# Moving the w turns, scans and gammas of units 4 and 5 into the first group's steps (RWKV-7 state recurrence with a hard-swish feed-forward)

## The chip, the cores and the metric

The kernel runs on one core of one Trainium2 chip. The metric is the device time of one execution in microseconds, the median of several runs.

## What is computed

The reference runs an RWKV-7 recurrence over 4 batches of 8 heads, 768 steps, head dimension 40, and puts its output through a two-layer feed-forward:

```python
for t in range(S):                       # state: (B, H, D, D), 0 at first
    y[:, :, t] = einsum('bhd,bhde->bhe', r_t, state)
    Sa = einsum('bhde,bhe->bhd', state, a_t)
    state = state * w_t[:, :, None, :] - einsum('bhd,bhe->bhde', Sa, b_t) \
            + einsum('bhd,bhe->bhde', v_t, k_t)
x = y as (B*S, H*D) = (3072, 320)
h = x @ w_in                             # (320, 2048)
out = (h * clip(h + 3, 0, 6) / 6) @ w_out   # (2048, 320)
```

## The kernel before

Time is cut into blocks of 64 steps. A **unit** is 128 rows: one block of two batches, eight heads each. There are 24 units; four of them (NU = 4) make a **group** of 128 steps for all batches. Units 0 to 3 are the first group, 4 to 7 the second.

For each unit `prepare(i, F)` gives the stages that don't need the state:

- `W`: four PE transposes of w into a PSUM bank, two copies of the halves into a tile `wm` (ACT; DVE for unit 0 alone), and a running product by a DVE scan (L544) into `prods`. It then fetches the next w of its tile.
- `gam`: reciprocal, a second DVE scan backwards (L555), and copies (DVE for units of later groups, POOL) that give the decay factors `gam`, their inverses `rgam` and `dec`. For units 4 to 8 it also fetches the unit's own v.
- `A`, `B`, `K`: turns of a, b, k, multiplied by `gam` or `rgam`; `factor`: k and b times the turned `rgam`; `F`, `E`, `EV`: products of these.

The F tiles of the group's units are inverted together, step by step on DVE (`invert`, L741 and L747), with `third_block` products at the end. `step(i)` gives the stages that use the inverse and the state: `RT`, `VT` (turns of r and v), `R`, `C`, `S`, `U`, `UT`, `rS`, `sn` (state update), `H`, `y`, and `move`, `move2`, which send the unit's result to its feed-forward tile `xt` by eight DMAs on SP.

A stage is a Python generator: its PE part is emitted, then it yields, then the rest (emptying the PSUM bank) is emitted. Between the two, other work can be dealt in. Each engine runs its own instructions in the order in which they are emitted; all DMAs spoken of here are emitted on SP's queue.

The w_in and w_out matrices come as 20 **weight pieces** that are converted before use (`load_weights`): per piece one to four load DMAs on SP (L328, into `raw` tiles and borrowed places), three ACT operations (L351, L353, L355) into one of two `parts` buffers, and three DVE operations (L372, L376, and L363, which writes the weight). A raw place can be loaded again only when an earlier piece is converted.

The order around the change is written out by hand. `PLAN` is a list of lines that run the first group's own steps: `2U:3` means stage U of unit 2, with three weight steps dealt between its PE part and the rest. `X` and `Y` are the third-block products of the inverse. From line 8 on, feed-forward **pieces** (`expand`, L1054, and `contract`, L1095) are emitted behind each line, and from line BEGIN = 10 on each line also takes one step of `second_group`, the stages of units 4 to 7 up to EV. `by_twos` deals these: in its step 0 come W of unit 4, W of unit 5, gam of 4, gam of 5, each followed by `pieces(0.625)`; step 1 has nothing; step 2 is A, step 3 is B of units 4 and 5 and W of 6 and 7. The tail of the plan reads:

```python
              3R:4 3VT                      # line 8
              2rS:3 2sn:3 2H:4 3S:2
              2y:3 3U:1 3UT:10 3C:5         # line 10
              3rS:1 3sn:2 3H:4 2move
              3y:1 2move2
```

PSUM tiles come from `ps_any` (a ring with the banks `one`, `pair` and at first `o`) and `ps_pair` (double banks, `pair` and at first `lent`); a stage waits until the last user of its bank has emptied it.

The w of unit 5 is loaded after line 8 into half of a tile (`WA1`) whose memory an earlier weight piece (raw_x) holds, together with its a (`seconds()`). Five tiles `values` hold v; unit i's v goes to `values[i % 5]`, so the fifth is first used by unit 4.

Of the kernel before, what the change touches and what calls it, by code (L numbers as in the profile page):

```python
# [8 lines left out]
F32 = mybir.dt.float32  # L9
# [22 lines left out]
def kernel(  # L32
# [152 lines left out]


    AHEAD = NU + 1
    PADS = {"W": 1.0}

    def padded(t, name):  # L190
        nc.gpsimd.memset(t[:, :, D:SLOT], PADS.get(name, 0.0))
        return t
# [32 lines left out]
        score.append(t)  # L225
    turn = [0]

    values = [padded(const.tile([P, H, SLOT], F32, name=f"V{i}"), "V") for i in range(AHEAD)]
    inputs["R"] = padded(const.tile([P, H, SLOT], F32, name="R"), "R")

    RR = const.tile([P, 2, NPR * D + SLOT - D], F32, name="RR")
# [202 lines left out]
    def fetch(name, i, engine=None):  # L434

        if i is None or i >= NK:
            return
        x, crossed = {"W": (w, 0), "A": (a, 0), "B": (b, 0), "K": (k, 0), "R": (r, 1),
                      "V": (v, 1)}[name]
        if name == "V":  # L440
            t = values[i % AHEAD]
        else:
            t = placed.get((name, i))
            if (name, i) == ("R", 1):
                t = others["K"]
            t = t if t is not None else (others if i < 2 * NU and i % 2 and name != "R" else inputs)[name]
        g, p = names[i]
        engines = engine or nc.sync
        for q in range(2):
            engine = engines[q] if isinstance(engines, tuple) else engines  # L450
            y = x[2 * p + q, :, g * BL:(g + 1) * BL, :]
            rows = slice(q * BL, (q + 1) * BL)
            if crossed:
                for s in range(2):
                    engine.dma_start(out=t[rows, 4 * s:4 * s + 4, 0:D],
                                     in_=y[s::2].rearrange("h t e -> t h e"))
            else:
                engine.dma_start(out=t[rows, :, 0:D], in_=y.rearrange("h t e -> t h e"))
        data[i][name + "N"] = t

    def following(i):

        if i < 2:
            return None
        if i < 2 * NU:

            return i + 2 if i % NU < NU - 2 or i % 2 == 0 else None
        return i + 1
# [55 lines left out]
    def prepare(i, F):  # L524
        n, o = i % NU, data[i]
        halves = i >= 2 * NU
        def w_stage():
            wt = turn_pairs(o["WN"])
            yield PE

            wm = o["wm"] = wms[i % 2]
            wv = wm[:, 0:SCAN].rearrange("p (r m i) -> p r m i", m=2, i=HB + 1)
            x = wt[:].rearrange("p r (q m i) -> p (r q) m i", q=2, m=2)
            if i == 0:
                nc.vector.tensor_copy(wv[:, :, 0, 1:HB + 1], x[:, :, 0, ::-1])
            else:
                nc.scalar.activation(out=wv[:, :, 0, 1:HB + 1], in_=x[:, :, 0, ::-1], func=AF.Copy)
            if i == 0:
                nc.vector.tensor_copy(wv[:, :, 1, 1:HB + 1], x[:, :, 1, :])
            else:  # L540
                nc.scalar.activation(out=wv[:, :, 1, 1:HB + 1], in_=x[:, :, 1, :], func=AF.Copy)  # L541
            fetch("W", following(i))
            prods = o["prods"] = tmp.tile([P, NB, 2, HB + 1], F32, name="prods", bufs=2)
            nc.vector.tensor_tensor_scan(  # L544
                out=prods[:].rearrange("p r m i -> p (r m i)"), data0=wm[:, 0:SCAN], data1=start[:],
                initial=0.0, op0=ALU.mult, op1=ALU.add,
            )

        def gam_stage():

            prods, wm = o["prods"], o["wm"]
            first = start[:].rearrange("p (n i) -> p n i", i=HB + 1)[:, :, 0]
            nc.vector.reciprocal(first, prods[:].rearrange("p r m i -> p (r m) i")[:, ::-1, HB])
            back = _ap(wm[:], SCAN, [[-1, SCAN]])
            nc.vector.tensor_tensor_scan(out=back, data0=back, data1=start[:], initial=0.0,  # L555
                                         op0=ALU.mult, op1=ALU.add)
            nc.vector.memset(first, 1.0)
            gam = o["G"] = grp.tile([P, NPR, P], F32, name="gam", tag="gam", bufs=NU + 2)
            rgam = o["rg"] = placed.get(("rgam", i)) or tmp.tile([P, NPR, P], F32, name="rgam", bufs=2)
            gv = gam[:].rearrange("p r (q i) -> p (r q) i", q=2)  # L560
            rv = rgam[:].rearrange("p r (q i) -> p (r q) i", q=2)
            row = 2 * (HB + 1)

            def copy(to, x):
                if i < NU:
                    nc.scalar.activation(out=to, in_=x, func=AF.Copy)
                else:
                    nc.vector.tensor_scalar(to, x, 1.0, None, ALU.mult)

            copy(gv[:, :, 0:HB], _ap(o["wm"][:], HB + 1, [[row, NB], [-1, HB]]))  # L570
            copy(rv[:, :, HB:BL], _ap(o["wm"][:], HB + 3, [[row, NB], [1, HB]]))
            nc.gpsimd.tensor_copy(gv[:, :, HB:BL], o["prods"][:, :, 1, 0:HB])  # L572
            nc.gpsimd.tensor_copy(rv[:, :, 0:HB], o["prods"][:, :, 0, 0:HB][:, :, ::-1])
            dec = grp.tile([P, 2, 2, NPR], F32, name="dec", tag="dec", bufs=NU + 2)
            nc.gpsimd.tensor_copy(dec[:].rearrange("p m q r -> p r q m"),
                                  o["prods"][:].rearrange("p (r q) m i -> p r q m i", q=2)[:, :, :, :, HB])
            o["dec"] = dec
            if NU <= i <= 2 * NU:
                fetch("V", i)
            yield from ()  # L580

# [120 lines left out]
    def in_turn(stages, order):  # L702

        for name in order:
            yield from stages[name]()
            shared[0] = None
            yield DONE

    def by_stages(i, stages):


        order = ["K", "factor", "F"] if i % NU < 2 else ["K", "F", "factor"]
        return in_turn(stages, ["W", "gam", "A", "B"] + order + ["E", "EV"])


    def invert(F, third, alone=False):
# [435 lines left out]
    def run(stage, steps=0, mixed=0, deals=0):  # L1152

        for at in stage:
            if at == DONE:
                return
            aside(steps, mixed)
            deal(deals)
# [17 lines left out]
    def by_twos(first, steps, mixed, rate):  # L1176


        chains = [by_stages(first + i, prepared(first + i)) for i in range(NU)]
        for t in range(TWOS):  # L1180

            order = [0, 1] if t < STAGES else []
            order += [2, 3] if t > 5 else []
            if t < 2:
                order = [0, 1, 0, 1][4 * t:]
            if t == 3:
                order = [2, 0, 3, 1]
            for i in order:
                run(chains[i], steps if t > 10 else 0, mixed)
                pieces(rate / 2)  # L1190
            if t == 10:
                side.append(invert(group_F[-1], third, first == 0))
            yield
# [16 lines left out]
    for n, x in enumerate(BESIDE):  # L1210
        limit[0] = {0: 4, 8: 12}.get(n, limit[0])
        while n == 0 and refill[0]():
            pass
        if n == 4:
            fetch("R", 0)
            fetch("R", 1)
        run(chains[int(x[0])], 1, MIXED if n >= 12 else 0)
    TURNS_IN = [("one", 1), ("pair", 2), ("pair", 2)]
    blocks = {}
# [26 lines left out]
    def block(i, j):  # L1246

        if i % NU < 2:
            if j == 0:
# [4 lines left out]


    PLAN = """X X:2 0U:4 0UT:2 1R
              0sn:2 0H:1 Y:2
              1U 1UT:2 0y
              2RT:1 Y:1
              1sn:1 1H:1 2VT:2 0move 0move2  # L1260
              1y:2 2R
              2S:3 3RT:2
              1move 1move2 2U:3 2UT:1 2C:5
              3R:4 3VT
# [9 lines left out]
    chains = {str(i): in_turn(stages[i], [x[0][1:] for line in plan for x in line if x[0][0] == str(i)])  # L1274
              for i in range(NU)}
    chains.update({x: firsts[n] for n, x in enumerate("XY")})
    for t, line in enumerate(plan):
        if t == 8:
            begun_ffn()
            ring.clear()  # L1280
            ring.extend([("one", 1), ("whole", 2)])
        for name, *amounts in line:
            run(chains[name[0]], 0, 0, *map(int, amounts))
        if t == 3:
            limit[0] = PIECES
        if t == BEGIN - 2:
            seconds()
            for name in "WA":
                fetch(name, NU + 1)
            third.clear()  # L1290
            second_group = by_twos(NU, 3, 0, 1.25)
        if t == BEGIN + 1:

            for name in "BK":
                others[name] = second(name)
                fetch(name, NU + 1)
        if t >= BEGIN - 2:
            pieces(3 if t < BEGIN else 1.5 if t < BEGIN + 3 else 0)
        if t >= BEGIN:
            next(second_group)  # L1300
# [156 lines left out]
```

## Time and profile before

| | |
|---|---|
| time, median of 3 runs | 798.12 us (797.23 to 798.37) |
| the profiled execution | span 802.0 us; no other time of it is given |
| mean granted TensorE clock | 0.956 |
| PE busy | 733.3 us (91%) |
| DVE busy | 495.5 us (62%) |
| ACT busy | 321.2 us (40%) |
| POOL busy | 175.6 us (22%) |
| L1054 and L1095 on PE, the feed-forward | 250.4 and 231.8 us |
| chain that ended last | PE 77%, DVE 8%, issue 5%, DMA 4%, SP's queue 2% |

All times of the profile are of one execution, counted from its first instruction. A row of the chain gives start, length and the engine and line that the end waited for; a row of the timeline gives start, length, engine, line, operation, output and inputs, and in brackets how long the engine had stood idle before it, with the releaser that the profile infers. "issue" means that the profile shows no releaser. PEld is PE's weight load, SPq the DMAs that SP issues. The first 140 us hold the first group; in them PE is busy 2 to 7 tenths.

### The profile page before, as it was taken

The page shows a single profiled execution, that of the slowest core. Times are in us where ns is not written, and L with a number is a line of the kernel's source. Part 1 is how long each engine was busy: PE and PEld are TensorE (multiplying, and loading weights), DVE is VectorE, ACT ScalarE, POOL GpSimd, SP SyncE. Part 2 cuts the span into 40 slices and gives each one's busy share as a digit, 9 for nine tenths or more (in the row PEclk, how much of TensorE's full clock was granted, in tenths as well). Part 3 has the DMA queues.
Part 4 walks back from the last instruction along what each step waited for, and adds up shares of the span by engine and source line. Part 5 has one row for each costly group of instructions (what it writes and reads, how often), then busy time and mean ns, then how long its engine had stood idle before and what let it go on. Part 6 is the DMA issues. An engine that isn't in the chain of part 4 may idle for free.

```text
span 802.0 us, 35325 instructions
## 1 busy us (share of the span) xinstructions
PE 733.3 (91%) x15832; PEld 622.8 (78%) x15832; DVE 495.5 (62%) x967; ACT 321.2 (40%) x668; POOL 175.6 (22%) x318
## 2 busy tenths in 40 slices
PE   5726777999999989999999999999999999999998
PEld 4625665878778868888888888888888888888886
DVE  7896777679555699455698445897444973322210
ACT  2348882321644424543344453324443324422111
POOL 6403012420322222223123123304122202000000
PEclk9855798999999999999999999999999999999999
DMA  9683553420233331233222233213222101110000
GB/s 120 118 198 85 152 142 57 76 46 9 45 57 66 59 56 28 53 64 56 41 45 43 44 58 62 46 34 57 44 51 48 20 20 29 30 25 13 15 19 17
DMA packets 174215, 45.03 MB, mean 56 GB/s; under 512 B 157424, under 2 KB 172784, under 8 KB 174064
## 3 DMA queue, kind: packets, MB, share of 16 engines
q1 hardware_dynamic: 169760, 42.03, 27.7%
q8 instruction: 125, 2.05, 1.1%
q10 hardware_dynamic: 4304, 0.74, 0.7%
q14 instruction: 26, 0.21, 0.1%
HBM read 34.08 MB, written 3.93 MB: 47 GB/s over the span
## 4 chain that ended last, share of the span: by engine, by line
PE 77%; DVE 8%; issue 5%; DMA 4%; SPq 2%; ACT 2%; POOL 1%; DVEq 0%; ACTq 0%; POOLq 0%
PE h L1054 26%; PE o L1095 24%; PE pair L512 4%; PE pair L972 3%; PE pair L484 2%; PE pair L949 2%; PE one L474 2%; PE pair L894 2%; PE pair L856 2%; PE pair L914 1%; PE pair L690 1%; PE pair L930 1%; DMA R<-in_r_dram 1%; DVE wm L555 1%; PE pair L799 1%
## 5 line engine op out<-in xcount | busy, mean ns | idle before, releaser
L1054 PE MATMUL h<-xt,win 128*128 128x128 f32 (+1 forms) x2304 | 250.4, 282 | 3.5 <-DVE gt L1070 3.5
L1054 PEld LDWEIGHTS h<-xt,win 128*128 128x128 f32 (+1 forms) x2304 | 230.8, 192 | 20.5 <-issue 4.2
L1095 PE MATMUL o<-wout,gt 128*128 128x320 f32 x768 | 231.8, 445 | 0.0
L1095 PEld LDWEIGHTS o<-wout,gt 128*128 128x128 f32 x768 | 139.2, 191 | 51.0 <-issue 1.2
L1070 DVE SCALAR_TENSOR_TENSOR gt<-gt,h 128x512 f32<-128x512 f32 x96 | 62.0, 681 | 71.7 <-ACT gt L1069 71.6
L1069 ACT ACTIVATE gt<-h,three 128x512 f32<-128x512 f32 x96 | 62.2, 686 | 100.9 <-PE h L1054 100.5
L984 POOL TENSOR_TENSOR yg<-ys,gam 128x512 f32<-128x512 f32 x22 | 39.0, 1772 | 165.4 <-DVE ys L983 91.2
L741 DVE TENSOR_TENSOR prod<-x 128x30 f32<-128x30 f32 (+9 forms) x180 | 67.2, 373 | 8.8 <-POOL x L726 3.3
L663 POOL TENSOR_TENSOR KBt<-K,rgt 128x320 f32<-128x320 f32 x22 | 19.0, 865 | 215.4 <-ACT rgt L652 166.9
L747 DVE TENSOR_TENSOR x<-x,prod 128x30 f32<-128x30 f32 (+9 forms) x180 | 62.3, 346 | 5.5
L957 DVE TENSOR_TENSOR state<-pair,state 40x320 f32<-40x320 f32 (+1 forms) x44 | 21.4, 487 | 65.9 <-PE pair L949 39.8
L520 DVE COPY_PREDICATED score<-mask,pair 128x512 f32<-128x512 int32 x71 | 49.9, 723 | 1.8 <-PE pair L512 1.4
L983 DVE TENSOR_TENSOR ys<-pair,ys 128x512 f32<-128x512 f32 x22 | 15.2, 691 | 44.7 <-PE pair L690 22.0
L555 DVE TENSOR_TENSOR_SCAN wm<-wm,start 128x528 f32<-128x528 f32 x24 | 37.6, 1565 | 0.8
L544 DVE TENSOR_TENSOR_SCAN prods<-wm,start 128x528 f32<-128x528 f32 x24 | 30.3, 1270 | 10.2 <-ACT wm L541 10.1
L834 ACT ACTIVATE RT<-pair 128x512 f32<-128x512 f32 x21 | 12.5, 597 | 52.9 <-PE pair L484 52.9
L972 PE MATMUL pair<-score,KBt 64*64 64x64 f32 x1472 | 29.2, 232 | 4.0 <-DVE state L957 3.2
L695 ACT ACTIVATE EV<-pair 64x320 f32<-64x320 f32 x44 | 19.0, 432 | 33.5 <-PE pair L690 22.8
L972 PEld LDWEIGHTS pair<-score,KBt 64*64 64x64 f32 x1472 | 25.8, 145 | 6.6 <-DVE state L957 3.7
L809 ACT ACTIVATE tinv<-pair 32x256 f32<-32x256 f32 x48 | 18.0, 375 | 30.1 <-PE pair L799 29.5
L1113 ACT ACTIVATE ob<-o 128x320 f32<-128x320 f32 x22 | 9.6, 435 | 49.1 <-PE o L1095 29.3
L572 POOL COPY gam<-prods 128x256 f32<-128x256 f32 x24 | 22.5, 937 | 29.3 <-DVE prods L544 25.4
(262 smaller groups left out, 1062.6 us busy)
## 6 DMA issues: line engine op xcount, KB each, us to landing
V<-in_v_dram SPq DMA_DIRECT2D x96, 40.0 KB
out_dram<-ob SPq DMA_DIRECT2D x47, 80.0 KB
R<-in_r_dram SPq DMA_DIRECT2D x92, 40.0 KB
B<-in_b_dram SPq DMA_DIRECT2D x42, 80.0 KB
K<-in_k_dram SPq DMA_DIRECT2D x42, 80.0 KB
W<-in_w_dram SPq DMA_DIRECT2D x37, 80.0 KB
A<-in_a_dram SPq DMA_DIRECT2D x37, 80.0 KB
xt<-yg SPq DMA_DIRECT2D x72, 40.0 KB
```

Source lines behind the costliest of these rows:

```text
L512: nc.tensor.matmul(out=o[i][half(q), n, :], lhsT=lhs[half(i, D), n ^ (2 * q * swap), half(q)], rhs=rhs[half(i, D), n, half(q)], start=True ...
L520: nc.vector.copy_predicated(out=x[:].rearrange("p (i h) t -> p i h t", i=2), mask=mask8, data=o[2])
L544: nc.vector.tensor_tensor_scan(out=prods[:].rearrange("p r m i -> p (r m i)"), data0=wm[:, 0:SCAN], data1=start[:], initial=0.0, op0=ALU.m ...
L555: nc.vector.tensor_tensor_scan(out=back, data0=back, data1=start[:], initial=0.0, op0=ALU.mult, op1=ALU.add)
L741: nc.vector.tensor_tensor(out=pv, in0=_ap(x[:], (i + 1) * L + i, [[L, n], [0, i]]), in1=_ap(x[:], i * L, [[0, n], [1, i]]), op=ALU.mult,)
L747: nc.vector.tensor_tensor(out=rest, in0=rest, in1=pv, op=ALU.add)
L972: nc.tensor.matmul(out=y[q][half(s), pr, :], lhsT=o[name][half(q), h * D:h * D + SLOT], rhs=m[name][half(q), 4 * rs + 2 * s + j, :], start ...
L984: nc.gpsimd.tensor_tensor(out=yg[:], in0=m["ys"][:].rearrange("p r q t -> p r (q t)"), in1=o["G"][:], op=ALU.mult)
L1054: nc.tensor.matmul(out=hp[c][:, i, :], lhsT=lhsT, rhs=rhs, start=(begun[c] == 0), stop=(begun[c] == 3 * NQ - 1))
L1069: nc.scalar.activation(out=gt[:], in_=hp[c][:], func=AF.Relu, bias=three[:], scale=1.0)
L1070: nc.vector.scalar_tensor_tensor(out=gt[:], in0=gt[:], scalar=6.0, in1=hp[c][:], op0=ALU.min, op1=ALU.mult)
L1095: nc.tensor.matmul(out=op[:], lhsT=gts[c][:, n, :], rhs=wout[:, c * HJ + r * NQ + n, :], start=((split or r == 0) and c == 0 and n == 0), ...
```

## The change

- W and gam of units 4 and 5 leave `by_twos` and become two chains, P and Q, in the plan: W of 4 at the end of line 1, gam of 4 at the end of line 2, W of 5 at the end of line 3, gam of 5 at the end of line 5. Step 0 of `by_twos` keeps only its feed-forward pieces.
- The two copies of the W stage of units 4 and 5 are done by DVE and no longer by ACT.
- The w of unit 5 goes into the fifth tile of v, and is loaded early, behind r of units 0 and 1. That tile's padding is therefore 1.0.
- The DMAs move with it: W of unit 6 is fetched in line 1, V of unit 5 in line 5 (with gam of 5). V of unit 4, A of unit 5 and W of unit 7 are fetched after line 8; before, W and A of unit 5 were fetched there, and W of 6 and 7 and V of 4 and 5 in step 0 of `by_twos`.

```diff
-    PADS = {"W": 1.0}
+    PADS = {"W": 1.0, "V4": 1.0}
...
+            if (name, i) == ("W", NU + 1):
+                t = values[NU]
...
-            if i == 0:
+            if i in (0, NU, NU + 1):
                 nc.vector.tensor_copy(wv[:, :, 0, 1:HB + 1], x[:, :, 0, ::-1])
...
-            fetch("W", following(i))
+            if i != NU + 1:
+                fetch("W", following(i))
...
-            if NU <= i <= 2 * NU:
+            if NU < i <= 2 * NU:
                 fetch("V", i)
...
+        scanned = [] if i < NU + 2 else ["W", "gam"]
...
-                run(chains[i], steps if t > 10 else 0, mixed)
+                if t >= 2 or first != NU:
+                    run(chains[i], steps if t > 10 else 0, mixed)
                 pieces(rate / 2)
...
             fetch("R", 1)
+            fetch("W", NU + 1)
...
     PLAN = """X X:2 0U:4 0UT:2 1R
-              0sn:2 0H:1 Y:2
-              1U 1UT:2 0y
-              2RT:1 Y:1
+              0sn:2 0H:1 Y:2 P
+              1U 1UT:2 0y P
+              2RT:1 Y:1 Q
               1sn:1 1H:1 2VT:2 0move 0move2
-              1y:2 2R
+              1y:2 2R Q
...
+    chains.update({x: in_turn(prepare(NU + n, None), ["W", "gam"]) for n, x in enumerate("PQ")})
...
         if t == BEGIN - 2:
             seconds()
-            for name in "WA":
-                fetch(name, NU + 1)
+            fetch("V", NU)
+            fetch("A", NU + 1)
+            fetch("W", NU + 3)
```

More of the change, by code (lines that the diff above doesn't have):

```diff
@@ L226 @@
     turn = [0]
-    values = [padded(const.tile([P, H, SLOT], F32, name=f"V{i}"), "V") for i in range(AHEAD)]
+    values = [padded(const.tile([P, H, SLOT], F32, name=f"V{i}"), f"V{i}") for i in range(AHEAD)]
     inputs["R"] = padded(const.tile([P, H, SLOT], F32, name="R"), "R")
@@ L537, in w_stage @@
                 nc.scalar.activation(out=wv[:, :, 0, 1:HB + 1], in_=x[:, :, 0, ::-1], func=AF.Copy)
-            if i == 0:
+            if i in (0, NU, NU + 1):
                 nc.vector.tensor_copy(wv[:, :, 1, 1:HB + 1], x[:, :, 1, :])
@@ L709, in by_stages @@
     def by_stages(i, stages):
+        scanned = [] if i < NU + 2 else ["W", "gam"]
         order = ["K", "factor", "F"] if i % NU < 2 else ["K", "F", "factor"]
-        return in_turn(stages, ["W", "gam", "A", "B"] + order + ["E", "EV"])
+        return in_turn(stages, scanned + ["A", "B"] + order + ["E", "EV"])
     def invert(F, third, alone=False):
```

## The prediction

> **What bounds the kernel now.** I read the slices of the page first. PE is at nine tenths or more from the eighth slice (140 us) on, with one 8 among them, and at 2 to 7 tenths before it, so what moves from behind that border to before it leaves a full engine for one with room. The change touches 50 to 138 us; I asked for the chain of waits from 60 to 140 us (start, length, what):
>
> ```profile
> 119.92 0.77 ACT parts L351
> ...
> 122.58 0.69 DVE wout L363
> 123.27 0.64 DVE score L520
> 123.92 2.30 DVE prods L544 x2
> ...
> 126.53 1.32 DVE wm L555
> ...
> 128.95 1.26 DVE wm L555
> ...
> 130.74 1.19 DVE gt L1070 x2
> 131.93 0.41 DVE state L957
> ...
> 132.39 1.98 PE pair L972 x64
> 134.37 4.18 PE o L1095 x8
> ```
>
> Two things end last here: the conversion of the feed-forward weights (L351 to L376, the last piece done at 123.27), and then the scans of units 4 and 5 on DVE, 123.92 to 130.74, in front of unit 3's state update, mask and product y. The timeline shows what PE does meanwhile (start, length, engine, line; idle before it in brackets):
>
> ```profile
> 122.10 0.58 ACT L920 ACTIVATE UT<-pair 128x512 f32<-128x512 f32 x1
> 122.77 0.63 PE L474 MATMUL pair<-ident,WA 128*128 128x128 f32 x4 [3.75 <-issue]
> 127.85 1.34 PE L1095 MATMUL o<-wout,gt 128*128 128x320 f32 x4
> 132.39 1.98 PE L972 MATMUL pair<-score,KBt 64*64 64x64 f32 x64 [3.19 <-DVE state L957]
> 134.30 4.25 PE L1095 MATMUL o<-wout,gt 128*128 128x320 f32 x8
> 138.39 0.60 PE L474 MATMUL one<-ident,A 128*128 128x128 f32 x4
> ```
>
> Unit 5's w turn waits 3.75 us until ACT has emptied unit 3's UT out of a `pair` bank (122.68), and ACT does that only after the ten weight steps dealt there. The product y waits 3.19 us for the scans. Eight L1095 then take 4.25 us, where another eight (at 150.56) take 2.42; the windows give a granted clock of 0.50 for 132 to 138 us.
>
> Last, SP's own timeline, because the change moves DMAs into it:
>
> ```profile
> 96.96 2.72 SPq L455 DMA_DIRECT2D R<-in_r_dram  x4
> 99.72 3.10 SPq L998 DMA_DIRECT2D xt<-yg  x4
> 102.87 3.51 SPq L1003 DMA_DIRECT2D xt<-yg  x4
> 106.48 0.52 SPq L328 DMA_DIRECT2D raw<-in_moe_w_out_dram  x1
> 107.11 1.36 SPq L458 DMA_DIRECT2D WA<-in_w_dram  x2
> 108.53 1.58 SPq L458 DMA_DIRECT2D WA<-in_a_dram  x2
> 110.21 1.34 SPq L328 DMA_DIRECT2D raw_fb<-in_moe_w_out_dram  x1
> ...
> 124.76 6.20 SPq L455 DMA_DIRECT2D V<-in_v_dram  x8
> ```
>
> From 81.69 (raw_x) to 113.2 us SP issues back to back, with gaps near 0.1 us. Weight piece 17 (raw_fb) is issued at 110.21, lands 4.51 us later (the chain), and ACT reads it at 115.54: under 1 us to spare.
>
> **What leaves 117 to 131 us.** Were everything earlier unmoved: unit 3's rS follows the emptying of UT, 122.7 + 0.69 = 123.4; sn needs the bank of the mask that ends at 123.92, two products of 0.65, so 125.2; H 0.69, 125.9; the four L1095 1.34, 127.3. Mask and state update, free of 6.8 us of scans, are done by 126.7. Product y starts at 127.3 instead of 132.39 (5.1 us earlier). At full clock y takes 1.69 (as at 112.93) and the eight L1095 2.42, so the turn of unit 4's a starts at 131.5 instead of 138.39: 6.9 us gained. The two turns themselves (0.6 us each) are in that figure. The feed-forward pieces that stood between them stay, 40 matmuls of about 0.13 us, and fill PE's wait. From 138 us PE is nearly solid up to 173 us, so I carry a shift there to the end one for one.
>
> **What arrives at 50 to 97 us.** Unit 5's w load is two DMAs (1.3 us, like L458) behind the R loads near 46 us; what it delays is used much later and the inversion on DVE covers it: 0 (1.3 us if that cover went). On PE: two turns of four at half clock, 0.66 to 1.11 us each (R at 80.28, V at 87.17); the first lies in a stretch that PE fills (72 to 81.9 us), so 1.0; the second can fall into the 2.7 us idle at 81.91. On ACT: nothing, the copies go to DVE, and four of 0.38 us leave ACT at 122.6. POOL gets six copies (0.3 to 1.4 us) in a stretch where it is nearly idle: 0; it loses them at 125 to 129, where unit 5's B and K pads stood behind them.
>
> On DVE per unit: copies 0.42 + 0.42 (rows of unit 0, L535 and L539), scan 1.26, reciprocal 0.25, scan 1.26, memset 0.07, copies 0.28 + 0.29: 4.25, together 8.5 us. Queue by queue in program order: unit 4's copies and scan hide in the 2.0 us idle ahead of L980 at 80.39, which comes 1.0 late through PE. Gam of 4 (2.15) then stands before L372, unit 2's scaling and L376, and unit 5's copies and scan before unit 1's state update: 82.1 + 2.15 + 1.6 + 2.1 = 88.0 against 86.40. The mask of 1H ends near 89.8 instead of 88.14, y and R of units 1 and 2 follow 1.7 late, and gam of 5 (2.15) stands before piece 8's L372: 95.3 instead of 91.27. Piece 8's L363 ends at 97.1, not 93.2; its `parts` buffer is what ACT needs for piece 10 at 94.14 (0.9 to spare): ACT is 3.0 late. The windows give ACT 5.84 to 5.87 us busy of each 6 from 90 to 108 us, so it doesn't catch up; with unit 2's U and UT between, some 3.6 late at the last pieces.
>
> On SP: W of unit 6 (1.3 us) fits the gap before raw_x. raw_x waits for the third block's product on PE, 1.1 late. Then four V DMAs for unit 5 (half of the 6.20 us row: 3.1) come ahead of piece 15, R, unit 1's moves and piece 16; four for unit 4 (3.1) and W of unit 7 in the place of unit 5's (0) ahead of pieces 17 to 19. Full price: 7.3 us; piece 17 lands at 122.0 instead of 114.7, and ACT's last conversions and the UT emptying behind them end 6.5 late. Some of it may be given back: one-DMA weight issues take 0.45 to 0.52 us (pieces 16, 18) but 1.30 and 1.34 at others (15, 17), and single moves 0.57 to 1.63, which suggests up to about 3 us of waiting that is absorbed.
>
> So the end of the conversions, and with it the 6.9 us, is put back by 3.6 (ACT alone) to 6.5 us (SP at full price). I take 5.0, a little nearer to the middle than to SP's end because of the uneven issues. Sum: −6.9 + 5.0 = −1.9 us. Against the profiled execution (span 802.0 us, the only figure of that execution) this is 800.1; the median of the runs, 798.12, is 3.9 below that span, and the shift is taken over unchanged: 796.2.
>
> **Rivals.** *The delay does not bite* (0.19): DVE's scans fall into idle times and SP's issues close up, so the conversions end only 1 to 2 us late; gain 5.5, time 792.6. For it: DVE is busy 2.41 of 6 us at 78 to 84 and 3.43 at 84 to 90. Against it: the back-to-back SP row.
>
> *Slower: the wait is moved ahead of rS and costs the clock* (0.26). If SP's price is paid in full, UT is emptied at about 129.2 (122.68 + 6.5), while PE, with C of unit 3 done near 119.7 (116.6 + about 3) and 40 feed-forward matmuls behind it (5.3), runs out of work near 125.0: 4 us idle in one piece. In this trace the 3.19 us wait at 129.2 was followed by clock 0.50 from 132 to 138, though the 3.75 us at 119 was not (clock 1.00 in the windows to 130). At half clock rS, sn and H (0.69 + 1.30 + 0.69 = 2.7) take 2.7 more: −6.9 + 6.5 + 2.7 = +2.3, 800.4. It decides from a delay of about 5.9 on, where 6.9 − 2.7 − delay leaves −1.6.
>
> The Trainium skill, "TensorE: Matmul & The Clock Gate", Part 1, states that the array falls to half clock after an idle window of about 3.4 us on a free-running clock, so that a wait of this length may or may not cause it. The two waits above, one with and one without a drop, agree with that; by the rule alone an idle of 4 us, given the full SP price, would mostly bring the drop, and the sum would be the 800.4 of this rival.
>
> *The wait only moves* (0.10): the full SP price but no drop of the clock, or a drop with less delay: −0.4, 797.7. That the change doesn't do what it says would look the same, with scans still between 123 and 131 us; the code gives no way to that, so it has no chance of its own.
>
> **How the numbers follow.** A measurement of this kernel can tell about 0.2%, 1.6 us. The forecast (0.45) spans delays of 3.6 to 6.5 us, 794.8 to 797.7, and about 1 us more on either side for the other terms: 0.31 faster, 0.12 same, 0.02 slower. With the rivals 0.19 faster, 0.26 slower and 0.10 same: 0.50, 0.22, 0.28. The range runs from 791.8 (a little beyond the first rival, short of the full 6.9) to 800.9 (just beyond the slower one).
>
> **What would show it.** In the changed kernel: no L544 or L555 between 123 and 131 us, but four pairs' worth between 76 and 96; V issues near 96 and 110 us on SP; raw_fb of L328 issued near 116 instead of 110.21; the last L363 ending near 128, UT (L920) right after it; y of unit 3 (L972) near 132 at the latest with no DVE wait before it; the eight L1095 in 2.4 us if the clock held; unit 4's a turn near 136.5. I am wrong if the conversions end before 125 (gain nearer 5), if PE's idle before rS is followed by clock 0.50 (loss), or if a shift at 138 us is not found again at the end.

## The result: 0.3% slower, and the profile after

| | before | changed |
|---|---|---|
| time, median of 7 runs | 798.21 us (797.23 to 799.13) | 800.35 us (798.94 to 802.92) |
| ratio to before | | 1.0034 (1.0018 to 1.0049) |
| profiled execution | span 802.0 us | span 798.6 us, time 800.6 us |

The changed kernel is slower in time and shorter in the profiled span. Both are true: the execution of before that was profiled was an unusually long one. The changed kernel's own profile puts 2.0 us outside its span; with as much, before's profiled execution took about 804 us, longer than any of its seven runs. The first experiment gives a second profile of before.

The stretch in question, from the timeline of the changed kernel (line numbers are 4 higher from L1054 on; L920 became L924, L930 became L934, y's L972 became L976, and the turns' L474 became L476):

```profile
116.86 4.04 PE L1058 MATMUL h<-xt,win 128*128 128x128 f32 x40
126.79 0.58 ACT L924 ACTIVATE UT<-pair 128x512 f32<-128x512 f32 x1
127.42 1.13 PE L934 MATMUL pair<-RT,S 40*64 40x64 f32 x32 [6.52 <-ACT UT L924]
131.07 2.50 PE L1099 MATMUL o<-wout,gt 128*128 128x320 f32 x4
134.97 2.42 PE L1099 MATMUL o<-wout,gt 128*128 128x320 f32 x8
137.23 0.60 PE L476 MATMUL one<-ident,A 128*128 128x128 f32 x4
```

No scan stands in front of unit 3's y any more, and the eight L1099 run at full speed. But unit 3's UT is emptied only at 126.79. PE has done its 40 feed-forward matmuls by 120.90 and waits 6.52 us in one piece; behind the wait rS (L934) takes 1.13 us and the four L1099 take 2.50, against 0.69 and 1.34 where before runs them at a clock of 1.00 (125.32 and 127.85 in its profile). SP's and ACT's timelines say why UT is late:

```profile
96.33 2.68 SPq L457 DMA_DIRECT2D V<-in_v_dram  x4
109.22 3.36 SPq L457 DMA_DIRECT2D V<-in_v_dram  x4
115.42 0.57 SPq L328 DMA_DIRECT2D raw_fb<-in_moe_w_out_dram  x1
120.28 0.77 ACT L351 ACTIVATE parts<-raw_fb,low 128x512 int32<-128x512 int16 x1 [4.10 <-DMA raw_fb<-in_moe_w_out_dram]
```

The two groups of V loads stand ahead of weight piece 17 on SP; it is issued at 115.42, and ACT stands idle 4.10 us until it lands.

### The profile page after: what moved, and what is told of

Same layout as the page of the kernel before. It is cut to its first block, busy times and chain, and to the rows that moved or that the text cites. A ratio compares the mean times of both kernels' runs of the same rounds, so it can differ in the third digit from the quotient of the medians.

```text
span 798.6 us, 35318 instructions
## 1 busy us (share of the span) xinstructions
PE 731.4 (92%) x15832; PEld 621.3 (78%) x15832; DVE 495.9 (62%) x971; ACT 320.0 (40%) x664; POOL 174.7 (22%) x318
## 4 chain that ended last, share of the span: by engine, by line
PE 72%; DVE 13%; issue 5%; DMA 4%; SPq 4%; ACT 2%; POOL 1%; DVEq 0%; ACTq 0%; POOLq 0%
PE h L1058 24%; PE o L1099 22%; PE pair L514 4%; PE pair L976 3%; DVE prod L745 3%; DVE x L751 3%; PE pair L953 2%; PE pair L486 2%; PE one L476 2%; SPq L460 2%; PE pair L898 2%; SPq L457 2%; PE pair L860 2%; PE pair L934 1%; PE pair L918 1%
## 5 line engine op out<-in xcount | busy, mean ns | idle before, releaser
L1099 PE MATMUL o<-wout,gt 128*128 128x320 f32 x768 | 230.8, 443 | 0.0
L1099 PEld LDWEIGHTS o<-wout,gt 128*128 128x128 f32 x768 | 138.7, 190 | 50.5 <-issue 0.4
L976 PE MATMUL pair<-score,KBt 64*64 64x64 f32 x1408 | 26.2, 223 | 0.2 <-issue 0.2
L864 DVE TENSOR_TENSOR RR<-pair,EV 128x320 f32<-128x320 f32 x22 | 10.7, 486 | 25.3 <-PE pair L514 25.3
```

Source lines behind the costliest of these rows:

```text
L976: nc.tensor.matmul(out=y[q][half(s), pr, :], lhsT=o[name][half(q), h * D:h * D + SLOT], rhs=m[name][half(q), 4 * rs + 2 * s + j, :], start ...
L1099: nc.tensor.matmul(out=op[:], lhsT=gts[c][:, n, :], rhs=wout[:, c * HJ + r * NQ + n, :], start=((split or r == 0) and c == 0 and n == 0), ...
```

## The experiments

All ratios are to the kernel before, run beside them on the same chip. "UT" is the start of the ACT operation that empties unit 3's UT, "a turn" the start of unit 4's a turn on PE, where the dense part begins; both from one profiled execution each.

| kernel | piece 17 issued | UT | a turn | span | ratio (95%) |
|---|---|---|---|---|---|
| before, first profile | 110.21 | 122.10 | 138.39 | 802.0 | |
| e1 before again | 108.52 | 120.28 | 135.79 | 797.2 | 0.9999 (0.9988 to 1.0010) |
| changed | 115.42 | 126.79 | 137.23 | 798.6 | 1.0034 (1.0018 to 1.0049) |
| e8 changed again | 115.43 | 127.11 | 136.89 | 799.1 | 1.0041 (1.0025 to 1.0057) |
| e2 scans early, V late | 110.02 | 122.42 | 132.06 | 792.4 | 0.9951 (0.9931 to 0.9970) |
| e3 V early alone | 116.23 | 127.89 | 141.36 | 803.2 | 1.0061 (1.0043 to 1.0078) |
| e6 V of 5 late only | 113.72 | 124.91 | 135.05 | 797.2 | 0.9988 (0.9972 to 1.0005) |
| e4 A and W late too | 107.87 | 121.91 | 131.50 | 793.9 | 0.9955 (0.9939 to 0.9972) |
| e10 copies on ACT | 110.04 | 122.07 | 131.70 | 794.0 | 0.9957 (0.9940 to 0.9974) |
| e5 gammas at lines 11, 12 | 110.31 | 121.77 | 132.49 | 796.3 | 0.9986 (0.9970 to 1.0002) |
| e7 changed, idle transposes | 116.31 | 127.78 | 135.48 | 797.8 | 0.9999 (0.9984 to 1.0013) |
| e9 e2, idle transposes | 110.77 | 123.99 | 132.05 | 796.9 | 0.9965 (0.9951 to 0.9980) |

**e1, the kernel before again** (no edit).

> The kernel before, unaltered, for a second profile of it. Its first profile has a span of 802.0 us, 3.9 us over the median of its runs, and the profile of the changed kernel a span of 798.6 us in an execution of 800.6 us, 2.0 us of it outside the span. Theory A (the first profile of before was an unlucky execution): the span is near 796 us, the 2.7 us idle of PE at 82 us in the midst of unit 1's sn is missing or much shorter, and unit 3's y (L972) starts 2 to 4 us earlier than 132.39. Theory B (the time around the span differs between the two kernels): the span is again near 802 us with the same stops at the same places. Time: 798.2 us, ratio 1.000 within 0.002 in both.

Its profiled execution took 798.97 us, of it 797.2 in the span: theory A. Its timeline has the same stops, but shorter or earlier (SP's line first):

```profile
108.52 0.57 SPq L328 DMA_DIRECT2D raw_fb<-in_moe_w_out_dram  x1
120.28 0.58 ACT L920 ACTIVATE UT<-pair 128x512 f32<-128x512 f32 x1
130.58 1.34 PE L972 MATMUL pair<-score,KBt 64*64 64x64 f32 x64 [1.66 <-DVE state L957]
135.79 0.60 PE L474 MATMUL one<-ident,A 128*128 128x128 f32 x4
```

PE's stop in unit 1's sn is 1.7 us, not 2.7; y starts 1.8 us earlier than in the first profile (I had said 2 to 4), and the a turn 2.6. Of the 4.8 us between the two spans these are 2.6; the rest is spread over the later part. This execution is the fastest of e1's twelve, 0.8 us under their median, so it is nearer to the middle than the first profile but not at it. Against it the changed kernel's a turn is 1.4 us late, and so is the end of its span.

**e2, scans early, V late**: the turns, scans and gammas as changed; the eight V loads behind line 10.

```diff
-            if NU < i <= 2 * NU:
+            if NU + 1 < i <= 2 * NU:
                 fetch("V", i)
...
-            fetch("V", NU)
             fetch("A", NU + 1)
...
+        if t == BEGIN:
+            fetch("V", NU)
+            fetch("V", NU + 1)
```

> The changed kernel with the eight DMAs of V of units 4 and 5 behind line 10 of the plan, where before has them, and all else as changed. SP theory (the V DMAs put back the last weight pieces, PE then idles 6.5 us before unit 3's rS and falls to half clock): raw_fb of L328 is issued near 110 us instead of 115.4, UT of unit 3 is emptied near 123 instead of 126.8, PE's idle before rS is under 3 us and rS, sn, H run at clock 1.0; time 794 to 796 us, faster than before by 2 to 4 us. DVE theory (the 8.5 us of scans and copies on DVE put back ACT's conversions whatever SP does): UT is still emptied after 125.5 us and the time stays at 799 to 801 us.

```profile
110.02 0.57 SPq L328 DMA_DIRECT2D raw_fb<-in_moe_w_out_dram  x1
122.42 0.58 ACT L924 ACTIVATE UT<-pair 128x512 f32<-128x512 f32 x1
123.05 0.69 PE L934 MATMUL pair<-RT,S 40*64 40x64 f32 x32 [2.17 <-ACT UT L924]
126.28 2.50 PE L1099 MATMUL o<-wout,gt 128*128 128x320 f32 x4
132.06 0.60 PE L476 MATMUL one<-ident,A 128*128 128x128 f32 x4
```

With SP relieved, the same early scans make the kernel 0.5% faster than before (795.0 us, median). The expectation held but for one point: even the 2.17 us wait was followed by half clock, on H and the four L1099.

**e3, V early alone**: before, with only the V loads at the changed kernel's places.

```diff
-            if NU <= i <= 2 * NU:
+            if NU + 1 < i <= 2 * NU:
                 fetch("V", i)
...
+        if t == 5:
+            fetch("V", NU + 1)
         if t == BEGIN - 2:
             seconds()
+            fetch("V", NU)
```

> The kernel before with only the eight V DMAs of units 4 and 5 moved to the places where the changed kernel has them (V of 5 behind line 5, V of 4 behind line 8); turns and scans stay. SP theory: raw_fb is issued 5 to 6 us later than in before, UT of unit 3 is emptied 4 to 5 us later and the whole kernel is 3 to 6 us slower (802 to 804 us). DVE theory: SP's delay is absorbed, 798 to 799 us.

```profile
116.23 0.57 SPq L328 DMA_DIRECT2D raw_fb<-in_moe_w_out_dram  x1
127.89 0.58 ACT L920 ACTIVATE UT<-pair 128x512 f32<-128x512 f32 x1
141.36 0.60 PE L474 MATMUL one<-ident,A 128*128 128x128 f32 x4
```

Piece 17 is issued 7.7 us later than in e1, UT is emptied 7.6 later (both more than expected), and the kernel is 0.6% slower. e2 (−0.49%) and e3 (+0.61%) add up to +0.12%; the whole change measures +0.34% (0.18 to 0.49). The two halves of the change are shown: the move of the scans gains, the move of the V loads loses about as much or a little more. Behind the early scans the V loads cost 0.83% (changed against e2), behind the late ones 0.61%; the intervals do not tell these two apart.

**e6, V of unit 5 late only**: as e2, with V of unit 4 left behind line 8.

> The changed kernel with only V of unit 5 behind line 10; V of unit 4 stays behind line 8. SP theory: raw_fb is issued 2.7 to 3 us earlier than 115.4, near 112.6, it lands near 117.3, piece 17 starts on ACT there, UT is emptied near 123.9 instead of 126.8, and the time lies between e2 (795.0) and the changed kernel (800.4), near 796.5 to 797.5. If the loss came from one of the two alone, it would be at one of the ends.

All places fall between those of e2 and of the changed kernel: piece 17 at 113.72 (1.1 later than I had said), UT at 124.91. The ratio lies between too. A group of four V DMAs takes 2.7 to 3.5 us to issue on SP; at the end of the conversions that of unit 4 costs 2.5 us here (UT against e2), and that of unit 5 another 1.9 (the changed kernel against this one). Here PE waits 4.40 us, and rS takes 1.13 us behind that wait too: the clock dropped with a delay of UT of only 4.6 us against e1.

**e7, the changed kernel with idle transposes**, to part the wait from the clock.

```diff
+        if t == BEGIN:
+            idle = bank("one", [P, 512], 1)
+            for _ in range(48):
+                nc.tensor.transpose(out=idle[:, 0:P], in_=ident[:], identity=ident[:])
```

> The changed kernel with 48 PE transposes of the identity into the free bank of units 4's turn, behind line 10's feed-forward pieces; their result is used by nobody. They fill some 5 us of PE's 6.5 us wait before unit 3's rS and change no other engine's work. Clock theory (the wait costs not only itself but half clock behind it): rS, sn and H take 0.69, 1.3 and 0.69 us instead of 1.13, 2.1 and 1.11, the four L1099 1.34 instead of 2.50, granted clock 1.0 from 126 to 134 us, and the kernel is 1.5 to 2.5 us faster than the changed one, about 798 to 799. If the half clock costs nothing because masks and state update end last there: 800.4 within 0.7.

The windows of the changed kernel, and then of e7, for the same 6 us (busy time of PE, PEld, DVE, ACT and POOL, granted clock, DMA share, GB/s):

```profile
126.00:132.00 6.00, 4.58 (x130) 4.27 (x131) 4.28 (x7) 3.08 (x6) 0.52 (x2) 0.50 0.19 31
```

```profile
126.00:132.00 6.00, 4.44 (x142) 3.54 (x140) 5.24 (x9) 3.94 (x7) 0.51 (x2) 1.00 0.18 29
```

```profile
128.41 0.69 PE L934 MATMUL pair<-RT,S 40*64 40x64 f32 x32 [1.37 <-ACT UT L924]
130.86 1.34 PE L1099 MATMUL o<-wout,gt 128*128 128x320 f32 x4
135.48 0.60 PE L476 MATMUL one<-ident,A 128*128 128x128 f32 x4
```

UT is emptied even a little later (127.78), the clock stays at 1.00, and the a turn comes 7.1 us after the emptying instead of 9.9 (9.2 in e8). Against before the ratio is 0.9999, against 1.0034 and 1.0041 for the changed kernel: work that nobody uses makes it 2.8 to 3.4 us faster by the ratios, somewhat more than expected. The profiles show 1.8 us of that at the a turn, with UT 1.0 us later, and 0.8 at the end of the span.

**e8, the changed kernel again** (no edit).

> The changed kernel, unaltered, beside the kernel before on one chip, for a second profile of it. SP theory: raw_fb issued near 115.5 to 116.5 us, UT of unit 3 emptied near 127, half clock for rS, sn and H behind a wait of 6 us, unit 4's a turn (first L476 on A) near 137 us, against 135.8 in the second profile of before; ratio to before 1.0034 again, within 0.0015. Rival (the 2 us were a matter of the chip or of the executions): ratio 1.000 or below and another place of the a turn.

It came as expected: UT at 127.11, the wait 6.03, the a turn at 136.89, the ratio 1.0041. The loss comes again in a second set of runs.

**e4, A of unit 5 and W of unit 7 behind line 10 as well** (on top of e2).

> The kernel of e2 with A of unit 5 and W of unit 7 behind line 10 as well, ahead of the V DMAs, so that nothing but weight loads and moves is on SP between line 8 and the last piece. If SP still sets the end of the conversions in e2: raw_fb issued near 106.6 us instead of 110.0, UT of unit 3 emptied 1 to 2 us earlier than 122.4, and 1 to 2 us faster than e2. If e2 is bound by ACT and DVE there (ACT reached piece 16 without waiting for its load): UT still near 122.4 and the time within 0.7 us of e2 (795.0).

Piece 17 is issued 2.2 us earlier than in e2, UT is emptied 0.5 us earlier, and the ratio is e2's. In e2, SP no longer sets the end of the conversions.

**e10, the copies of the two turns on ACT** (on top of e2).

> The kernel of e2 with the two copies of the w turns of units 4 and 5 on ACT, as in before, and not on DVE. Theory that ACT and DVE together set the remaining 2 us (ACT full from 90 to 111 us, DVE late by its scans): four copies of 0.38 us more on ACT between 77 and 87 us, where ACT still has some idle, and 1.7 us less on DVE; UT emptied between 121.5 and 123.5, time within 1 us of e2. If ACT's queue were the bound from 77 us on: UT 1.5 us later and 1 to 2 us slower than e2.

UT 122.07, ratio 0.9957: on which engine these copies run makes no difference that these runs could tell. PE's wait (2.17 us) and the slow four L1099 behind it (2.12) are there as in e2.

**e5, gam of units 4 and 5 at the ends of lines 11 and 12** (on top of e2).

> The kernel of e2 with the gam stages of units 4 and 5 taken from lines 2 and 5 to the ends of lines 11 and 12, where e2 leaves DVE idle for 2.9 us ahead of unit 3's y and 2 us behind it; the turns and first scans stay early. DVE theory of the rest of the price (the two gammas, 4.3 us of DVE, put back ACT's pieces by 1.5 to 2 us): ACT's piece 10 at 93.6 to 94 instead of 95.16, UT emptied near 121 instead of 122.4, 1 to 2 us faster than e2, 793 to 794 us. Rival (DVE's early work is free, the 2 us come from elsewhere): UT stays at 122.4 and the time is that of e2 or up to 1 us more for the gammas behind line 12.

Half a miss. ACT's piece 10 starts at 93.16 instead of 95.16, so the gammas on DVE were what held it up; but UT comes only 0.65 us earlier, because piece 16, waiting for its load, gives the rest back (111.45 against 112.38 in e2). The time is worse than e2's by 0.35%. The profile shows 0.4 us of loss against e2 at the a turn, where the gamma of unit 5 now stands before its a, and 2.3 us by 200 us (by the starts of DVE's gt operations); where that second part goes was not tracked down.

**e9, e2 with 18 idle transposes.**

> The kernel of e2 with 18 unused PE transposes of the identity behind line 10's feed-forward pieces, to fill its 2.2 us wait before unit 3's rS. Clock theory: H (1.11 us in e2) and the four L1099 (2.50) run at full clock, 0.69 and 1.34, and the a turn comes 1 to 1.5 us earlier than 132.06; time 0.5 to 1.5 us below e2's ratio of 0.9951, so 0.993 to 0.9945. Rival (mask and state update of unit 3 end last in e2, or the transposes outlast the wait): the ratio is e2's or up to 1 us worse.

Within the stretch it did what it should: H 0.67, the four L1099 1.34, and 7.5 us from the emptying of UT to the a turn against 9.1 in e2. But in its profile UT was emptied 1.6 us later than in e2, and PE lost some 3.6 us against e1 between 163 and 621 us; the ratio, 0.9965, is not better than e2's. Why the gain doesn't arrive is open.

## Why the prediction was wrong

The forecast was −1.9 us; the likeliest case was wrong, and the rival "slower" (800.4) is what happened. The step that failed is the clock: the forecast put its drop behind PE's wait at nothing and priced it only in that rival. The delay of the conversions was also taken too small. Against e1, and with e7 for the full clock, the three terms can be read off:

- *What leaves 117 to 131 us*: forecast −6.9. From the emptying of UT (its end) to the a turn e1 takes 14.9 us, e7 7.1: −7.8. The mechanism holds, and the size to within 0.9.
- *The clock*: forecast 0, measured 2.7 us (9.9 us from the emptying to the a turn, against 7.1 in e7), in e8 2.1. The forecast let the feed-forward pieces fill PE's wait: C of unit 3 was to be done near 119.7 and the 40 matmuls behind it near 125.0. They started at 116.86, took 4.04 us and were done at 120.90 (121.7 in e8). So even the forecast's own delay of 5.0 would have left PE idle for 5 us or more, and e6 has the drop behind 4.40 us, e2, e4 and e10 behind 2.2. e7 is the test: with the wait filled the clock stays at 1.00, and the ratio goes from 1.0034 and 1.0041 to 0.9999. That the rival too had priced the drop at 2.7 us is chance: it laid all of it on rS, sn and H, which lost 1.2 us against e7; the four L1099 lost another 1.2 and y 0.4.
- *The delay of the conversions*: I took 5.0 from a span of 3.6 to 6.5. Against e1 it measures 6.5 (126.79 against 120.28), 6.8 in e8; against the first profile of before it is 4.7, so its size is known no better than the 1.8 us between the two profiles. I had taken the uneven issue times on SP (0.52 against 1.30 us) for waiting that could be absorbed, and so went below SP's full price. In e1 the two long issues, pieces 15 and 17, take 0.52 and 0.57 us, and SP is simply earlier: the unevenness belonged to that execution. Issue of piece 17 was put back 6.9 us against e1, beside the full price of 7.3.

So −7.8 + 6.5 + 2.7 = +1.4 us at the a turn (137.23 against 135.79). This sum must close, since its terms are read from the same places; that the spans differ by the same 1.4 (798.6 against 797.2) is the check. By the runs' medians it is 2.1, by the ratio 2.7 with an interval of 1.4 to 3.9. With the forecast's other terms, the delay of 6.5 alone would have given −0.4; the clock's 2.7 alone would have given +0.8, the other sign.

The second failure is the baseline: "the shift is taken over unchanged". My a turn of 136.5 was 0.7 us from the measured one, and the measured delay against the first profile, 4.7, looks like my 5.0. But that profile's a turn at 138.39 was itself 2.6 us later than e1's. That the place came out nearly right is luck as well: from the emptying to the a turn I had 8.8 us at full clock, which takes 7.1 at full clock and took 9.9. The page showed a sign of the baseline, a span 3.9 us over the median of the times.

Smaller points. DVE's and ACT's part of the delay, forecast as 3.6, is 2.1 where it nearly stands alone (e2 against e1; 1.6 in e4, with SP freer still): piece 8's L372 came at 92.85 in the changed kernel, not 95.3, because unit 0's y was done at 80.46 in spite of the turn ahead of it and DVE started its gamma earlier. That the copies cost nothing on either engine agrees with e10; the PE and POOL costs put at nothing were not tested alone. The early load of unit 5's w shifts the loads behind it by 1.3 us as forecast, and no longer wait shows behind them. Three slips in my working change nothing in the sum: the slices have a second 8, the last of them; 91.27 + 1.7 + 2.15 is 95.1, not 95.3; and the scans of the two units between 76 and 96 us are four, two pairs.

The Trainium skill, "TensorE: Matmul & The Clock Gate", Part 1, puts the drop to half clock behind an idle window of about 3.4 us. The drop behind the 6.5 us wait agrees; the one behind e2's wait of 2.17 us came sooner than that.

## What to carry to other kernels

When a step is moved earlier, price the loads that it takes along on the queue into which they go, as carefully as its arithmetic: here two groups of four loads, some 3 us of issue each ahead of a late weight piece, cost 0.8%, and leaving them where they were turned +0.3% into −0.5%. SP issued back to back for 30 us, and of the 7.3 us reckoned as its full price 6.9 arrived at piece 17: in such a place, reckon with the full price. Where a step is taken out ahead of a wait, work out when PE runs out of work, and reckon with the clock too. And compare the profiled execution's span with the times before subtracting anything from it; with differences of 0.3%, take a second profile of the kernel before.

## What had not been expected of the hardware

Filling PE's wait with work that nobody uses paid in one of two kernels: in e7, 48 transposes kept the granted clock at 1.00 and saved some 3 us by the ratios; in e9, 18 kept it at 1.00 from 120 to 130 us and saved 1.6 us in the stretch, but nothing in the time. How long a wait must be for the drop is not fixed in these traces: 3.75 us at 119 us in the first profile of before had none (clock 1.00 to 130 us), the same wait in e1, 3.76 us, had one (0.92 and 0.50 in the windows from 120 to 124 us), and so had 2.17 us in e2 (0.82 and 0.50 in the windows from 124 to 128 us). And executions of one kernel, the one before, ranged from 797.2 to 802.9 us, with single DMA issues of the same shape on SP between 0.52 and 1.30 us.
